# New step costs, a delay for each engine and later weight landings in the list schedule of an experts' stage

## The chip, the core and the metric

The kernel runs on one core of one Trainium2 chip. The metric is the time of one launch on the device, in microseconds (us). Before the change three runs took 1431.03, 1432.60 and 1433.58 us; the median is 1432.6 us. The execution that was profiled is the one of 1433.58 us.

## The reference

Three parts follow each other: linear attention, a layer of eight experts with fixed capacity, and a wide feed-forward layer. All of it is float32.

```python
q_s = softmax(q, axis=-1); k_s = softmax(k, axis=2)          # (8, 8, 576, 64)
kv  = einsum('bhsd,bhse->bhde', k_s, v)
x   = einsum('bhsd,bhde->bhse', q_s, kv) -> reshape (4608, 512)

logits = x @ w_gate                                          # 4608 x 8
for idx in argsort(-logits.flatten()):                       # greedy, best pair first
    tok, e = idx // 8, idx % 8
    if assigned[tok] >= 0 or counts[e] >= 576: continue
    assigned[tok] = e; counts[e] += 1
for e in range(8):
    out[assigned == e] = maximum(x[assigned == e] @ w1[e], 0) @ w2[e]   # 512 -> 1024 -> 512

h = out @ w_in                                               # 512 -> 2048
y = (h * tanh(softplus(h))) @ w_out                          # 2048 -> 512
```

The greedy assignment fills the experts one after another: each expert ends up with exactly 576 tokens.

## The kernel before, in words

Three stages stand behind each other in time: attention with the first list of tokens (to about 170 us of the span), the eight experts (about 172 to 670 us), and the feed-forward layer, called block 2 here (from about 660 us to the end). The change concerns the experts' stage.

**What the experts' stage does.** For each expert a list of its 576 tokens must be found, its tokens gathered from HBM, transposed and multiplied.

- `route(ph)` makes the list of expert `ph`. It is one long chain between VectorE (DVE) and TensorE (PE): six rounds, each of a compare on DVE (`cmp`, tile `cm`), 18 small matmuls that count (L868), two DVE instructions for flags, one matmul that broadcasts (L879), and two DVE instructions. Then `place`, `onehot`, 18 matmuls (L792), four matmuls (L807), and `ids`, which writes the list `ix` (L812, L814). Lists 1 to 7 are made in this stage, while earlier experts are multiplied. Expert 0's list is made in the attention stage.
- `load_x(ph)` gathers the tokens by the list in five indirect DMAs, issued by GpSimd (POOL) (tile `xg`, L952), transposes each on PE (four matmuls, tile `tp`, L963) and splits the result into a high part (ScalarE, ACT, L969) and a low part (DVE, L973), tile `xT`. There is one PSUM buffer `tp`, so a transposition can't start before the low part of the one before is made.
- `load_expert(ph)` gathers the weights in eight indirect DMAs on POOL (tile `wst`, four buffers, L924) and splits each half into high (ACT, L905) and low (DVE, L911), tile `unit`.
- `expert(ph)` is the bulk of PE's work: 16 hops of 24 matmuls each, 128x288 out. Each hop's result goes through ACT (`hh`, L1001) and DVE (`hh`, L1005), and back to PE (`yp`, L1013). ACT also writes the result out (`ys`, L1020).
- `convert_w` rewrites the weights of block 2 (from 64-bit words to high and low parts) on ACT and DVE and stores them in HBM with DMAs from SyncE's queue (SP; L1211, L1240), in gaps of the same stage.

**What sets the order.** Class `Sched` takes every step of the stage with an engine, a cost in us, its reads and writes, a priority and a count of buffers. `run()` (L92) plays a clock: it takes the step that can start first (ties by priority), books its engine for `cost`, and lets its readers start `lat` later. The Python functions of the steps are called in that order, so the clock's order is the order of instructions in each engine's queue. An engine takes its queue strictly in that order: an instruction that waits holds all that stand behind it. No time of this clock is in the program; it only sets the order.

- `lat` is one number in this stage before: 0.259 us. A DMA from SP has 2.53 us, a gather its own `lat=` (tokens 5.0 us, weights 5.5 us; expert 0: 3.0 and 4.0).
- `keep` (0.332 before): if a step of low priority on DVE or ACT would be taken, and a step of high priority would become ready within `keep` times its cost, the latter is taken instead (L115 to L121).
- `slack` adds to the ready time of a step: 0.3 us for PE's steps of `route`.

The last 17 steps of the experts and block 2 have schedulers of their own.

Of the kernel before, what the change touches and what calls it, by code (L numbers as in the profile page):

```python
# [23 lines left out]
NJ = NT // 128  # L24
# [12 lines left out]

LISTS = 5.7


class Sched:
# [39 lines left out]
    def run(self, free=()):  # L81
# [28 lines left out]
        while ready:  # L110
# [497 lines left out]
class Moe:  # L608
# [17 lines left out]
    def route(self, ph, bank):  # L626
# [76 lines left out]
        def rows():  # L703
# [4 lines left out]
            if not last:  # L708
                V.tensor_tensor(c["act"], c["act"], T["est"], op=OP.subtract)
        dve(0.7, expert, r=["acc", ("act", 0)] + allv + ([] if last else [f"nb{NR - 1}"]), w=["est"])  # L710

        def select():
# [8 lines left out]
            V.scalar_tensor_tensor(sel[:, 1], T["x"][:, :, 0], T["ns"], cs, op0=OP.is_equal, op1=OP.mult)  # L721
        dve(0.8, select, r=["est", "acc"] + allv, w=["sel"])
        dve(0.6, rows, r=["est"], w=["wi", ("act", 0)])

# [50 lines left out]
        def pay():  # L775
# [5 lines left out]
            for a in range(2):  # L781
                V.tensor_tensor(P[:, :, a], b, two(c["thl"][:, a])[:, :, None, :].to_broadcast(sh), op=OP.mult)
        dve(1.1, pay, r=["qr"], w=["P"])
        CH = [(0, 9), (9, 18)] if ph == 0 else [(0, 18)]
        for g0, g1 in CH:
            dve(0.08 + 0.073 * (g1 - g0), lambda g0=g0, g1=g1: onehot(g0, g1), r=["qr"], w=["A%d" % g0] + (["A"] if g0 == 0 else []))

# [7 lines left out]
        for g0, g1 in CH:  # L795
            pe(0.03 * (g1 - g0), lambda g0=g0, g1=g1: lists(g0, g1), r=["A", "A%d" % g0, "P"], w=["ls"],
               new=["ls"] if g0 == 0 else [])
# [12 lines left out]
        def ids():  # L810
# [3 lines left out]
            V.scalar_tensor_tensor(ix, T["sp"][:, 0:5], 64.0, lh, op0=OP.mult, op1=OP.add)  # L814
        dve(0.22, flat, r=["ls"], w=["iv"])
        pe(0.15, spread, r=["iv"], w=["sp"], new=["sp"])
        dve(0.38, ids, r=["sp"], w=["ix"])

# [12 lines left out]
        if not last:  # L831
            def done():
                V.scalar_tensor_tensor(L, T["est"][:, None, :].to_broadcast([128, NJ, E]), -BIG, L,
                                       op0=OP.mult, op1=OP.add)
            p += 5
            dve(0.5, done, r=["est"] + (["ix"] if ph == 0 else []), w=[("L", 0)] + ([("L", j) for j in range(1, NJ)] if ph == 0 else []))

    def keep_list(self, ph):
        self.sc.op("POOL", 0.6, self.keep[ph], r=[("ix", ph)], w=[("gl", ph)], prio=0, slack=0.0 if ph else LISTS + 10.0)

    def round(self, ph, T, n, dve, pe, bank, cuts, allw, allv):
# [47 lines left out]
        for j0, j1 in CH:  # L889
            dve(0.16 + 0.00053 * NT_ * (j1 - j0), lambda j0=j0, j1=j1: cmp(j0, j1), r=["w%d" % j0, "cm"][:2 if j0 else 1] if first else allw + ["cm"] * (j0 > 0) + ["acc"] * (n > 0) + [("ls", ph - 1)] * (n == 0 and ph > 0),  # L890
                w=["cm%d" % j0] + ["cm"] * (j0 == 0), early=first and j1 < NJ)
# [24 lines left out]
    def load_expert(self, ph, w1, w2, xd):  # L916
# [11 lines left out]
        for which, rows in (("w1", w1r), ("w2", w2r)):  # L928
            for g in range(4):
                key = (which, ph, g)  # L930
                first = ph == 0 and which == "w1"
                sc.op("POOL", 1.1, lambda w=which, g=g, r=rows: weight(w, g, r),
                      r=[("wi", ph)] + ([("xg", 0, 4)] if ph == 0 and which == "w2" else []), w=[key],
                      new=[("wst", key)], prio=-2001 if first else p, lat=4.0 if first else 5.5)
                for q in range(2):
# [10 lines left out]
    def load_x(self, ph, xd):  # L946
# [28 lines left out]
        for t in range(5):  # L975
            n = 128 if t < 4 else 64
            xg, tp, xt = ("xg", ph, t), ("tp", ph, t), ("xt", ph, t)
            sc.op("POOL", 1.1 if ph else 1.25, lambda t=t, n=n: gather(t, n), r=[("ix", ph), "xd"], w=[xg], new=[("xg", xg)],
                  prio=p, lat=5.0 if ph else 3.0, slack=0.0 if ph else LISTS)
            sc.op("PE", 0.45 if ph else 0.85, lambda t=t, n=n: tr(t, n), r=[xg], w=[tp], new=[("tp", tp)] if ph or t == 4 else [], prio=p)  # L980
            sc.op("ACT", 0.61, lambda t=t, n=n: hi(t, n), r=[tp] + ([("xT", ph)] if t else []), w=[xt] + ([("xT", ph)] if t == 0 else []),
                  new=[("xT", ("xT", ph))] if t == 0 else [], prio=p)
            sc.op("DVE", 0.7, lambda t=t, n=n: low(t, n), r=[tp, xt, ("xT", ph)], w=[xt], prio=p)

    def expert(self, ph, yd):
# [50 lines left out]
        for hf in range(2):  # L1036
            for f in range(8):
                hp, hh = ("hp", ph, hf, f), ("hh", ph, hf, f)

                def hop(hf=hf, f=f, hp=hp, hh=hh):  # L1040
# [5 lines left out]
                    over = ph == E - 1 and hf == 1 and f >= 8 - OVER  # L1046
                    self.sc.op("ACT", 0.43, lambda: h_hi(hf, f), r=[hp], w=[hh], new=[("unit" if over else "hh", hh)], prio=-5000)
                    self.sc.op("DVE", 0.47, lambda: h_lo(hf, f), r=[hp], w=[hh], prio=-5000)

                def yop(hf=hf, f=f, hh=hh):  # L1050
# [10 lines left out]
                    elif f == 7:  # L1061
                        for d in range(4):
                            self.sc.op("ACT", 0.43, lambda d=d: y_out(hf, d), r=[yp] + ([("ys", ph, hf)] if d else []),
                                  w=[("ys", ph, hf, d)] + ([("ys", ph, hf)] if d == 0 else []),
                                  new=[("ys", ("ys", ph, hf))] if d == 0 else [], prio=-4000)
# [77 lines left out]
    def convert_w(self, w_in, w_out, wdo, wdi):  # L1143
# [9 lines left out]
        def load(key, src, behind=(), unit=False):  # L1153
# [16 lines left out]
            p, gate = when()  # L1170
            sc.op("DMA", 2.6, ld, r=gate, w=[k64], new=[("w64", k64)], prio=p, lat=4.0)
            sc.op("ACT", 0.69, size, r=[k64] + list(behind), w=[cv], new=[("unit" if unit else "cv", cv)], prio=p)
            for step in range(3):
                sc.op("DVE", (0.45, 0.72, 0.72)[step], lambda step=step: bits(step), r=[k64], w=[cv], prio=p)
            return cv

        def split(cv, key, store, done):
# [13 lines left out]
            count[0] += 1  # L1191
            sc.op("ACT", 0.66, hi, r=[cv], w=[uw], new=[("unit", uw)] if cv != uw else [], prio=p)
            sc.op("DVE", 0.71, low, r=[cv, uw], w=[uw], prio=p)
            sc.op("DMA", 2.6, lambda: store(T["uw", key]), r=[uw], w=[done], prio=p)

        def combine(name, out, a, b, op, fresh=False):
# [349 lines left out]
def attention_moe_ffn(ctx, tc, q, k, v, w_gate, w1, w2, w_in, w_out, out):  # L1546
# [106 lines left out]
```

## Time and profile before

| | |
|---|---|
| median of three runs | 1432.6 us |
| the profiled execution, its own time | 1433.58 us |
| its span, first to last instruction | 1431.8 us |
| mean granted TensorE clock | 0.975 |
| PE busy, DVE busy, ACT busy, POOL busy | 94%, 73%, 55%, 19% |
| matmuls | 10256 |

The profile page gives the busy share of each engine, and the queries of the trace give rows for stretches of the span. PE's busy time runs from a matmul's start to a modelled end, so matmuls that follow each other overlap. A busy PE is therefore not PE at its peak; what tells more is the idle time in front of an instruction, which a row gives in brackets with what ended it. The granted clock stands in each stretch as a share of 2.4 GHz; 0.5 is the lower level, 1.2 GHz. In the order of instructions times don't occur at all; they are read from the trace.

### The profile page before, as it was taken

Reading aid. Unit: us, or ns where it says so; the run is one execution under the profiler, and the core shown is the slowest. Engines: PE = TensorE matmul, PEld = TensorE weight load, DVE = VectorE, ACT = ScalarE, POOL = GpSimd, SP = SyncE. Lnnn points to the kernel's source line nnn. Section 1 sums busy time; section 2 is a strip of 40 time slices with the busy share of each in tenths; the row PEclk is TensorE's granted clock in tenths of the full one; section 3 lists DMA queues with packets and bytes.
Section 4 is the critical chain, followed back from the end, with each engine's and each line's share of the span. In section 5 each row is a group of like instructions: output and inputs, shape, how many; then the busy total and the mean of one; then the engine's idle time right before and its main releaser. Section 6 shows DMA issues by size and latency. Waiting matters only on the chain.

```text
span 1431.8 us, 26732 instructions
## 1 busy us (share of the span) xinstructions
PE 1344.6 (94%) x10256; PEld 1244.2 (87%) x10256; DVE 1046.1 (73%) x2207; ACT 790.8 (55%) x1513; POOL 277.1 (19%) x314
## 2 busy tenths in 40 slices
PE   4987399999999789998999999999999999999997
PEld 4877298999999789998889989899898998999996
DVE  7897768887878757746787686776768677786764
ACT  4675224343344336434666666666666666675663
POOL 7896213312322231100001010000101001010101
PEclk9999599999999889999999999999999999999999
DMA  9997325555556668767966676675658556665650
GB/s 259 268 259 282 129 61 169 171 169 153 161 185 195 202 204 274 243 210 251 351 199 216 185 216 180 203 241 177 213 173 256 175 185 206 212 210 171 202 169 30
DMA packets 161919, 286.98 MB, mean 200 GB/s; under 512 B 25600, under 2 KB 101376, under 8 KB 161792
## 3 DMA queue, kind: packets, MB, share of 16 engines
q1 hardware_dynamic: 137680, 222.35, 51.1%
q0 software_dynamic: 15040, 52.44, 11.1%
q10 hardware_dynamic: 9072, 10.49, 2.1%
q8 instruction: 81, 1.33, 0.4%
q14 instruction: 46, 0.38, 0.1%
HBM read 235.95 MB, written 49.28 MB: 199 GB/s over the span
## 4 chain that ended last, share of the span: by engine, by line
PE 55%; issue 30%; DMA 5%; DVE 5%; POOL 2%; ACT 2%; SPq 1%; ACTq 0%; POOLq 0%; DVEq 0%
PE hp L994 13%; PE yp L1013 12%; PE yp L1479 12%; PE hp L1353 11%; PE rt L868 2%; DMA kh<-in_k_dram 2%; POOL out_dram L1491 2%; DMA wst<-in_moe_w_dram,wi 2%; PE tp L963 1%; PE xp L429 1%; DMA xg<-xd,ix 1%; DVE km L244 1%; DMA v<-in_v_dram 1%; DMA q<-in_q_dram 0%; DVE cm L856 0%
## 5 line engine op out<-in xcount | busy, mean ns | idle before, releaser
L1479 PE MATMUL yp<-unit,g 128*128 128x512 f32 x1728 | 431.3, 392 | 0.1
L1479 PEld LDWEIGHTS yp<-unit,g 128*128 128x128 f32 x1728 | 309.9, 188 | 56.4 <-DVE g L1391 1.0
L1353 PEld LDWEIGHTS hp<-yTa,unit 128*128 128x128 f32 x2256 | 288.3, 188 | 18.6 <-DVE hp L1442 2.9
L1353 PE MATMUL hp<-yTa,unit 128*128 128x256 f32 x2256 | 294.0, 279 | 4.1 <-DVE hp L1442 2.7
L994 PE MATMUL hp<-xT,unit 128*128 128x288 f32 x1536 | 284.7, 303 | 4.2 <-DVE hh L1005 3.5
L1013 PE MATMUL yp<-hh,unit 128*128 128x288 f32 x1500 | 266.6, 297 | 0.0
L994 PEld LDWEIGHTS hp<-xT,unit 128*128 128x128 f32 x1536 | 229.8, 191 | 5.3 <-DVE hh L1005 4.1
L1013 PEld LDWEIGHTS yp<-hh,unit 128*128 128x128 f32 x1500 | 222.2, 189 | 0.4 <-ACT ys L1020 0.2
L1491 POOL DMA_INDIRECT out_dram<-os,gix x36 | 38.6, 1073 | 793.8 <-ACT os L1487 454.6
L1001 ACT ACTIVATE hh<-hp 128x288 fp32r<-128x288 f32 x125 | 51.3, 411 | 199.3 <-PE hp L994 183.3
L1361 ACT ACTIVATE u<-hp 128x512 f32<-128x512 f32 x144 | 86.1, 598 | 117.7 <-PE hp L1353 112.4
L1378 DVE SCALAR_TENSOR_TENSOR u<-w,r 128x512 f32<-128x512 f32 x144 | 98.7, 687 | 45.5 <-ACT r L1375 44.9
L1388 ACT ACTIVATE g<-w 128x512 fp32r<-128x512 f32 x144 | 90.3, 627 | 74.8 <-DVE w L1384 74.0
L924 POOL DMA_INDIRECT wst<-in_moe_w_dram,wi x64 | 66.7, 1043 | 259.4 <-DVE unit L911 54.1
L1005 DVE SCALAR_TENSOR_TENSOR hh<-hp,hh 128x288 fp32r<-128x288 f32 x125 | 56.6, 455 | 71.1 <-ACT hh L1001 70.9
L905 ACT ACTIVATE unit<-wst 128x512 fp32r<-128x512 f32 x128 | 77.9, 645 | 55.5 <-DMA wst<-in_moe_w_dram,wi 51.1
L1391 DVE TENSOR_TENSOR g<-w,g 128x512 fp32r<-128x512 f32 x144 | 98.8, 686 | 5.6 <-ACT g L1388 4.1
L1384 DVE SCALAR_TENSOR_TENSOR w<-r,hp 128x512 f32<-128x512 f32 x144 | 98.3, 683 | 5.5
L1353 PEld LDWEIGHTS hp<-yTb,unit 128*128 128x128 f32 x768 | 99.1, 191 | 3.5
L1353 PE MATMUL hp<-yTb,unit 128*128 128x256 f32 x768 | 102.1, 282 | 0.0
L1381 DVE SCALAR_TENSOR_TENSOR r<-u,r 128x512 f32<-128x512 f32 x144 | 98.8, 687 | 1.9
L1364 DVE TENSOR_SCALAR u<-u 128x512 f32<-128x512 f32 x144 | 61.0, 425 | 51.0 <-ACT u L1361 50.4
(205 smaller groups left out, 1724.1 us busy)
## 6 DMA issues: line engine op xcount, KB each, us to landing
unit<-wdi SPq DMA_DIRECT2D x216, 512.0 KB, 4.2
unit<-wdi SPq DMA_DIRECT2D x72, 256.0 KB, 3.9
wdi<-unit SPq DMA_DIRECT2D x56, 256.0 KB, 3.4
yd<-ys ACTq DMA_DIRECT2D x15, 576.0 KB, 5.2
k<-in_k_dram SPq DMA_DIRECT2D x16, 512.0 KB, 6.4
q<-in_q_dram SPq DMA_DIRECT2D x16, 512.0 KB, 7.0
v<-in_v_dram SPq DMA_DIRECT2D x32, 256.0 KB, 6.3
xd<-xs SPq DMA_DIRECT2D x16, 512.0 KB, 4.4
```

The costliest lines, as they stand in the source:

```text
L905: nc.scalar.activation(f, v, AF.Copy)
L994: MM(t, u[:, a, 128 * (f % 4):128 * (f % 4) + 128], x[:, b, k, HALF * hf:HALF * hf + HALF], start=(k == 0 and n == 0), stop=(k == 3 and n ...
L1013: MM(T["yp", ph, hf][d], u[:, a, 128 * d:128 * d + 128], t[:, b], start=(f == 0 and n == 0), stop=(f == 7 and n == 2))
L1353: MM(dst, u[:, h, a, kk], y[:, b, kk], start=first, stop=False, skip_group_check=True)
L1361: nc.scalar.activation(t, T[zp], AF.Exp)
L1378: V.scalar_tensor_tensor(T[u], T[w], 1.0, T[rk], op0=OP.add, op1=OP.mult)
L1381: V.scalar_tensor_tensor(T[rk], T[u], 2.0, T[rk], op0=OP.subtract, op1=OP.mult)
L1384: V.scalar_tensor_tensor(T[w], T[rk], 0.5, T[zp], op0=OP.add, op1=OP.mult)
L1388: nc.scalar.activation(t[:, 0], T[w], AF.Copy)
L1391: V.tensor_tensor(T[g][:, 1], T[w], T[g][:, 0].bitcast(F32), op=OP.subtract)
L1479: MM(T["op", c, t], g[:, a, 128 * t:128 * t + 128], u[:, b], start=(i == 0 and n == 0), stop=(i == 15 and n == 2))
L1491: at = nc.gpsimd.indirect_dma_start(out=out, out_offset=bass.IndirectOffsetOnAxis(ap=gix[:, 4 * c + t:4 * c + t + 1], axis=0), in_=T["os", ...
```

## The change

It replaces numbers that `Sched` reckons with, in the experts' stage. `lat` becomes a table by engine (PE 0.23, DVE 0.14, ACT 0.16, POOL 0.25), `keep` goes from 0.332 to 1.0, the costs of the steps on DVE, ACT and PE become smaller by 0.04 to 0.3 us (a few become larger: the gathers on POOL from 1.1 to 1.25 us, the first DVE steps of lists 1 to 7), and the landing of a weight gather goes from 5.5 to 8.0 us. The landing of a token gather stays at 5.0 us. The steps themselves, their instructions, buffers and priorities stay as they are. The schedules of the attention stage and of block 2 give the same order of instructions as before. The diff, cut to its core:

```diff
+LAT = {"PE": 0.23, "DVE": 0.14, "ACT": 0.16, "POOL": 0.25}
+KEEP = 1.0
...
-            done = e + (lat if lat is not None else 2.53 if eng == "DMA" else self.lat)
+            done = e + (lat if lat is not None else 2.53 if eng == "DMA" else self.lat if isinstance(self.lat, float) else self.lat[eng])
...
-            dve(0.7 + 0.05 * (j1 - j0), lambda ...: sel_first(j0, j1), ...
+            dve(0.7 + 0.05 * (j1 - j0) if ph == 0 else 2.28, lambda ...: sel_first(j0, j1), ...
...
-        dve(1.7, place, r=["sl", "unsel"], w=["qr", ("fs", 0)])
+        dve(1.45, place, r=["sl", "unsel"], w=["qr", ("fs", 0)])
...
-        dve(0.33, flags, r=[c4], w=[fl])
-        pe(0.15, bcast, r=[fl], w=[nb], new=[nb])
-        dve(0.5 if n + 1 < NR else 0.18, accum, r=[nb] + allw, w=["acc"])
+        dve(0.28, flags, r=[c4], w=[fl])
+        pe(0.06, bcast, r=[fl], w=[nb], new=[nb])
+        dve(0.4 if n + 1 < NR else 0.1, accum, r=[nb] + allw, w=["acc"])
...
-        sc.op("ACT", 0.66, hi, r=[key], w=[unit, hk], new=[("unit", unit)], prio=prio)
-        sc.op("DVE", 0.71, low, r=[key, hk, unit], w=[lk], prio=prio)
+        sc.op("ACT", 0.56, hi, r=[key], w=[unit, hk], new=[("unit", unit)], prio=prio)
+        sc.op("DVE", 0.61, low, r=[key, hk, unit], w=[lk], prio=prio)
...
-                sc.op("POOL", 1.1, lambda w=which, g=g, r=rows: weight(w, g, r), ...
-                      new=[("wst", key)], prio=-2001 if first else p, lat=4.0 if first else 5.5)
+                sc.op("POOL", 1.25, lambda w=which, g=g, r=rows: weight(w, g, r), ...
+                      new=[("wst", key)], prio=-2001 if first else p, lat=4.0 if first else 8.0)
...
-                    self.sc.op("ACT", 0.43, lambda: h_hi(hf, f), ...
-                    self.sc.op("DVE", 0.47, lambda: h_lo(hf, f), ...
+                    self.sc.op("ACT", 0.32, lambda: h_hi(hf, f), ...
+                    self.sc.op("DVE", 0.38, lambda: h_lo(hf, f), ...
...
-    sc = m.sc = Sched(slots, 0.259, 0.332)
+    sc = m.sc = Sched(slots, LAT, KEEP)
```

Line numbers of the changed kernel are four higher than those of the kernel before, from L43 on.

**Two places in the order.** The first is ACT's queue around the transpositions of list 1 (`xT`), the weight splits (`unit<-wst`), the results of expert 0 that are written out (`ys`), and the converted weights of block 2 (`cv`). Before:

```order
L1020 ACTIVATE ys<-yp_2759 128x288
L905 ACTIVATE unit<-wst 128x512
L1020 ACTIVATE ys<-yp_2760 128x288
L1020 ACTIVATE ys<-yp_2761 128x288
L1020 ACTIVATE ys<-yp_2762 128x288
L969 ACTIVATE xT<-tp 128x4x128
L1028 DMA yd_61<-ys 128x4x288
L905 ACTIVATE unit<-wst 128x512 x4
L969 ACTIVATE xT<-tp 128x4x128
```

The same list in the changed kernel, on the same engine, from its first transposition to its last:

```order
L973 ACTIVATE xT<-tp 128x4x128
L1097 ACTIVATE cv<-w_2911 128x512
L1005 ACTIVATE hh<-hp 128x288
L973 ACTIVATE xT<-tp 128x4x128 x2
L909 ACTIVATE unit<-wst 128x512
L1005 ACTIVATE hh<-hp 128x288
L909 ACTIVATE unit<-wst 128x512 x5
L973 ACTIVATE xT<-tp 128x4x128
L973 ACTIVATE xT<-tp 128x4x64
```

The transpositions of list 1 stood between and behind the `ys` of expert 0 and the splits of the weights. Now three of the five stand ahead of those splits, and the `ys` have moved away behind them.

The second is PE's queue at list 6, from its last matmuls (L807) to the transposition of the first tokens gathered by it (L963). Before:

```order
L807 LDWEIGHTS lst
L807 MATMUL rt<-iv,lst 128x10
L994 MATMUL hp<-xT,unit 128x288 x3
L1013 MATMUL yp_6585<-hh,unit 128x288 x3
L1013 MATMUL yp_6586<-hh,unit 128x288 x3
L735 LDWEIGHTS tri
L735 MATMUL rt<-rk,tri 128x2
L736 LDWEIGHTS irt
L736 MATMUL rt<-rk,irt 128x1
L963 MATMUL tp<-ident,xg 128x128 x4
```

In the changed kernel list 6 is made some 50 us of matmuls earlier, and 11.6 us of matmuls stand between its L811 and its first transposition. Its second and third transposition, in the hops of expert 5, with all that lies between:

```order
L967 MATMUL tp<-ident,xg 128x128 x4
L998 MATMUL hp<-xT,unit 128x288 x3
L1017 MATMUL yp_6755<-hh,unit 128x288 x3
L998 MATMUL hp<-xT,unit 128x288 x3
L1017 MATMUL yp_6752<-hh,unit 128x288 x3
L998 MATMUL hp<-xT,unit 128x288 x3
L1017 MATMUL yp_6753<-hh,unit 128x288 x3
L998 MATMUL hp<-xT,unit 128x288 x3
L1017 MATMUL yp_6754<-hh,unit 128x288 x3
L967 MATMUL tp<-ident,xg 128x128 x4
```

Before, nine matmuls of the experts and two small ones lay between list and transposition, and none of the experts' matmuls between the first and the second transposition of list 6. Now 24 of them lie between one transposition and the next.

## Rows read from the trace of the kernel before

**Rows 1.** The page, part 4: the chain that ended last, by engine.

```profile
PE 55%; issue 30%; DMA 5%; DVE 5%; POOL 2%; ACT 2%; SPq 1%; ACTq 0%; POOLq 0%; DVEq 0%
```

**Rows 2.** Windows of 10 us: busy us by engine (instructions), clock, DMA share, GB/s.

```profile
230.00:240.00 10.00, 9.65 (x109) 8.88 (x108) 8.01 (x21) 3.87 (x8) 7.16 (x7) 1.00 0.69 220
240.00:250.00 10.00, 7.63 (x72) 6.98 (x69) 7.56 (x19) 6.36 (x14) 0.00 (x0) 0.83 0.37 136
...
330.00:340.00 10.00, 7.95 (x64) 7.50 (x63) 6.17 (x14) 2.20 (x5) 7.28 (x7) 0.83 0.70 197
...
490.00:500.00 10.00, 1.94 (x26) 1.67 (x24) 6.36 (x18) 2.27 (x5) 6.80 (x6) 0.68 0.83 279
500.00:510.00 10.00, 8.63 (x48) 7.70 (x49) 9.15 (x18) 5.40 (x11) 4.78 (x6) 0.64 0.48 137
510.00:520.00 10.00, 7.47 (x57) 7.23 (x57) 3.87 (x8) 2.21 (x5) 6.14 (x7) 1.00 0.88 292
520.00:530.00 10.00, 10.00 (x65) 10.00 (x66) 7.77 (x14) 3.99 (x8) 1.87 (x2) 0.83 0.86 294
530.00:540.00 10.00, 10.00 (x78) 10.00 (x77) 1.42 (x4) 2.93 (x9) 0.00 (x0) 1.00 0.08 31
```

**Rows 3.** The same view, one window of 50 us.

```profile
250.00:300.00 50.00, 50.00 (x465) 48.63 (x464) 41.19 (x107) 19.84 (x42) 13.63 (x15) 1.00 0.51 163
```

**Rows 4.** Waits in 180 to 670 us: total us, times, longest.

```profile
PE tp L963 <- DMA xg<-xd,ix: 9.3, 2, 7.3
...
PE hp L994 <- DVE hh L1005: 3.5, 2, 2.5
...
ACT unit L905 <- DMA wst<-in_moe_w_dram,wi: 20.5, 13, 7.6
```

**Rows 5.** PE by time: start, us, instruction, in brackets idle before, releaser.

```profile
243.10 0.66 PE L963 MATMUL tp<-ident,xg 128*128 128x128 f32 x4 [1.60 <-DVE xT L973]
...
325.45 0.26 PE L807 MATMUL rt<-iv,lst 128*128 128x10 bf16 x4
...
336.63 1.12 PE L963 MATMUL tp<-ident,xg 128*128 128x128 f32 x4 [2.05 <-DMA xg<-xd,ix]
...
488.48 0.26 PE L807 MATMUL rt<-iv,lst 128*128 128x10 bf16 x4
...
497.33 1.11 PE L963 MATMUL tp<-ident,xg 128*128 128x128 f32 x4 [7.25 <-DMA xg<-xd,ix]
...
519.84 0.66 PE L994 MATMUL hp<-xT,unit 128*128 128x288 f32 x3 [2.53 <-DVE hh L1005]
```

**Rows 6.** ACT in order of time, at the stall of 241 us.

```profile
240.30 0.63 ACT L905 ACTIVATE unit<-wst 128x512 fp32r<-128x512 f32 x1 [0.72 <-DMA wst<-in_moe_w_dram,wi]
...
241.71 0.61 ACT L969 ACTIVATE xT<-tp 128x512 fp32r<-128x512 f32 x1
```

**Rows 7.** POOL by time, before token gathers of lists 3 and 6.

```profile
330.30 0.18 POOL L823 COPY gix<-ix 64x4 int32<-64x4 int32 x1 [3.11 <-DMA wst<-in_moe_w_dram,wi]
...
489.91 1.29 POOL L952 DMA_INDIRECT xg<-xd,ix  x1 [0.39 <-PE yp L1013]
```

**Rows 8.** Token gathers (L952): us from issue to landing.

```profile
DMA to landing us min/median/max: 3.1/4.1/8.4
```

**Rows 9.** Weight gathers (L924): the same.

```profile
DMA to landing us min/median/max: 4.1/5.4/8.7
```

**Rows 10.** The chain in order of time: start, us, piece.

```profile
252.34 0.65 PE rt L868 x18
...
255.99 0.79 PE yp L1013 x6
```

**Rows 11.** DVE in order of time: runs of equal instructions.

```profile
182.22 0.81 DVE L1005 SCALAR_TENSOR_TENSOR hh<-hp,hh 128x288 fp32r<-128x288 f32 x2
...
502.25 1.89 DVE L911 TENSOR_TENSOR unit<-wst,unit 128x512 fp32r<-128x512 f32 x3
```

**Rows 12.** SP by time: the last store of converted weights.

```profile
623.38 10.64 SPq L1240 DMA_DIRECT2D wdo<-unit  x2
```

More of the change, by code (lines that the diff above doesn't have):

```diff
@@ L709, in rows @@
                 V.tensor_tensor(c["act"], c["act"], T["est"], op=OP.subtract)
-        dve(0.7, expert, r=["acc", ("act", 0)] + allv + ([] if last else [f"nb{NR - 1}"]), w=["est"])
+        dve(0.6, expert, r=["acc", ("act", 0)] + allv + ([] if last else [f"nb{NR - 1}"]), w=["est"])
         def select():
@@ L795, in route @@
         for g0, g1 in CH:
[L796 removed]
+            pe(0.027 * (g1 - g0), lambda g0=g0, g1=g1: lists(g0, g1), r=["A", "A%d" % g0, "P"], w=["ls"],
                new=["ls"] if g0 == 0 else [])
@@ L835, in route @@
             p += 5
-            dve(0.5, done, r=["est"] + (["ix"] if ph == 0 else []), w=[("L", 0)] + ([("L", j) for j in range(1, NJ)] if ph == 0 else []))
+            dve(0.36, done, r=["est"] + (["ix"] if ph == 0 else []), w=[("L", 0)] + ([("L", j) for j in range(1, NJ)] if ph == 0 else []))
     def keep_list(self, ph):
-        self.sc.op("POOL", 0.6, self.keep[ph], r=[("ix", ph)], w=[("gl", ph)], prio=0, slack=0.0 if ph else LISTS + 10.0)
+        self.sc.op("POOL", 0.7, self.keep[ph], r=[("ix", ph)], w=[("gl", ph)], prio=0, slack=0.0 if ph else LISTS + 10.0)
     def round(self, ph, T, n, dve, pe, bank, cuts, allw, allv):
@@ L931, in load_expert @@
                 first = ph == 0 and which == "w1"
-                sc.op("POOL", 1.1, lambda w=which, g=g, r=rows: weight(w, g, r),
+                sc.op("POOL", 1.25, lambda w=which, g=g, r=rows: weight(w, g, r),
                       r=[("wi", ph)] + ([("xg", 0, 4)] if ph == 0 and which == "w2" else []), w=[key],
-                      new=[("wst", key)], prio=-2001 if first else p, lat=4.0 if first else 5.5)
+                      new=[("wst", key)], prio=-2001 if first else p, lat=4.0 if first else 8.0)
                 for q in range(2):
@@ L980, in load_x @@
             sc.op("PE", 0.45 if ph else 0.85, lambda t=t, n=n: tr(t, n), r=[xg], w=[tp], new=[("tp", tp)] if ph or t == 4 else [], prio=p)
-            sc.op("ACT", 0.61, lambda t=t, n=n: hi(t, n), r=[tp] + ([("xT", ph)] if t else []), w=[xt] + ([("xT", ph)] if t == 0 else []),
+            sc.op("ACT", 0.5 if t < 4 else 0.3, lambda t=t, n=n: hi(t, n), r=[tp] + ([("xT", ph)] if t else []), w=[xt] + ([("xT", ph)] if t == 0 else []),
                   new=[("xT", ("xT", ph))] if t == 0 else [], prio=p)
-            sc.op("DVE", 0.7, lambda t=t, n=n: low(t, n), r=[tp, xt, ("xT", ph)], w=[xt], prio=p)
+            sc.op("DVE", 0.61 if t < 4 else 0.35, lambda t=t, n=n: low(t, n), r=[tp, xt, ("xT", ph)], w=[xt], prio=p)
     def expert(self, ph, yd):
@@ L1046, in hop @@
                     over = ph == E - 1 and hf == 1 and f >= 8 - OVER
-                    self.sc.op("ACT", 0.43, lambda: h_hi(hf, f), r=[hp], w=[hh], new=[("unit" if over else "hh", hh)], prio=-5000)
-                    self.sc.op("DVE", 0.47, lambda: h_lo(hf, f), r=[hp], w=[hh], prio=-5000)
+                    self.sc.op("ACT", 0.32, lambda: h_hi(hf, f), r=[hp], w=[hh], new=[("unit" if over else "hh", hh)], prio=-5000)
+                    self.sc.op("DVE", 0.38, lambda: h_lo(hf, f), r=[hp], w=[hh], prio=-5000)
                 def yop(hf=hf, f=f, hh=hh):
@@ L1062, in yop @@
                         for d in range(4):
-                            self.sc.op("ACT", 0.43, lambda d=d: y_out(hf, d), r=[yp] + ([("ys", ph, hf)] if d else []),
+                            self.sc.op("ACT", 0.31, lambda d=d: y_out(hf, d), r=[yp] + ([("ys", ph, hf)] if d else []),
                                   w=[("ys", ph, hf, d)] + ([("ys", ph, hf)] if d == 0 else []),
@@ L1170, in load @@
             p, gate = when()
-            sc.op("DMA", 2.6, ld, r=gate, w=[k64], new=[("w64", k64)], prio=p, lat=4.0)
-            sc.op("ACT", 0.69, size, r=[k64] + list(behind), w=[cv], new=[("unit" if unit else "cv", cv)], prio=p)
+            sc.op("DMA", 1.8, ld, r=gate, w=[k64], new=[("w64", k64)], prio=p, lat=5.0)
+            sc.op("ACT", 0.58, size, r=[k64] + list(behind), w=[cv], new=[("unit" if unit else "cv", cv)], prio=p)
             for step in range(3):
-                sc.op("DVE", (0.45, 0.72, 0.72)[step], lambda step=step: bits(step), r=[k64], w=[cv], prio=p)
+                sc.op("DVE", (0.36, 0.62, 0.62)[step], lambda step=step: bits(step), r=[k64], w=[cv], prio=p)
             return cv
@@ L1191, in split @@
             count[0] += 1
-            sc.op("ACT", 0.66, hi, r=[cv], w=[uw], new=[("unit", uw)] if cv != uw else [], prio=p)
-            sc.op("DVE", 0.71, low, r=[cv, uw], w=[uw], prio=p)
-            sc.op("DMA", 2.6, lambda: store(T["uw", key]), r=[uw], w=[done], prio=p)
+            sc.op("ACT", 0.54, hi, r=[cv], w=[uw], new=[("unit", uw)] if cv != uw else [], prio=p)
+            sc.op("DVE", 0.61, low, r=[cv, uw], w=[uw], prio=p)
+            sc.op("DMA", 1.8, lambda: store(T["uw", key]), r=[uw], w=[done], prio=p)
         def combine(name, out, a, b, op, fresh=False):
@@ L1201, in combine @@
             p, _ = when()
-            sc.op("DVE", 0.71, go, r=[a, b], w=[out], new=[("cv", out)] if fresh else [], prio=p)
+            sc.op("DVE", 0.61, go, r=[a, b], w=[out], new=[("cv", out)] if fresh else [], prio=p)
         def part(cv, what, q, kk):
```

26 lines of the change are left out of this document (13 added, 13 removed).

## The prediction, made before the changed kernel was run

> **What bounds the kernel now.** I read the page's chain first: PE carries 55% of what ended last and "issue" 30%, DVE and ACT together 7% [rows 1]. A chain so full of PE says that the time is PE's work plus the holes in it, so the second view is the one of windows, 10 us at a time through the experts' stage. In a good window PE is busy for all 10.00 us at a granted clock of 1.00 with 78 matmuls, as in 530 to 540 [rows 2]. Seven others are not. Per window I count as lost the idle time, and of the busy time the part that the clock withheld, (10 − busy) + busy × (1 − clock):
>
> - 230 to 240: 0.35; 240 to 250: 2.37 + 7.63 × 0.17 = 3.67
> - 330 to 340: 2.05 + 7.95 × 0.17 = 3.40
> - 490 to 500: 8.06 + 1.94 × 0.32 = 8.68; 500 to 510: 1.37 + 8.63 × 0.36 = 4.48
> - 510 to 520: 2.53; 520 to 530: 10.00 × 0.17 = 1.70
>
> The sum is **24.8 us**, all from [rows 2]. In each case the clock falls below 1.00 only in a window with a hole or in the one behind it, so I treat it as part of the hole's price.
>
> Third, the waits of the stage tell who makes the holes. PE's transpositions wait for tokens for 9.3 us in two waits; ACT's weight splits wait for gathered weights for 20.5 us in 13, up to 7.6 [rows 4]. Then the engines in order of time, hole by hole:
>
> - **Hole A, 238 to 243.** ACT waits for a weight gather before a split [rows 6]. Behind that split, in ACT's queue, stand the results of expert 0 and the split of list 1's transposition, so PE's next transposition starts only at 243.10, 1.60 us late [rows 5].
> - **Hole B, 334 to 337.** List 3 leaves PE at 325.45, its first transposition waits 2.05 us for its tokens [rows 5]. POOL held them up: the copy in front of the token gathers waited 3.11 us for the landing of a weight gather [rows 7].
> - **Hole C, 490 to 510.** List 6 leaves PE at 488.48, POOL issues its first gather at 489.91, and PE, whose queue has next to nothing before the transposition, stands idle for 7.25 us [rows 5, 7]. The transpositions then follow each other at the low clock.
> - **Hole D, 517 to 520.** 2.53 us before a hop whose `hh` is late [rows 5], which is again queued behind late weights.
>
> **The change, part by part.** No instruction is added or removed, and nothing changes in attention, or in block 2 except when its first work can start. So the sum is made of which hole the new order closes, and which it opens. Distances in the order I turn into time with the trace's own durations: six 288-column matmuls take 0.79 us, 0.132 each, and 18 counting matmuls 0.65 [rows 10].
>
> *Lists earlier, and gathers with room.* From a list's last matmuls to its first transposition there lie, lists 1 to 7, 8.1, 9.3, 8.9, 8.5, 8.1, 1.3 and 7.3 us of PE work before and 8.1, 8.1, 8.9, 9.3, 8.1, 11.6 and 50.5 us now. What is needed is 1.43 us to the issue (488.48 to 489.91 [rows 5, 7]) and a landing of 3.1, 4.1 or 8.4 us (minimum, median, maximum [rows 8]), so 4.5, 5.5 or 9.8. List 6, with 1.3, had to fail; with 11.6 it is safe even at the maximum. That closes hole C. It is also made some 48 us of PE work earlier, and list 7 39 us earlier. Hole B closes for another reason. Its distance doesn't grow, but the copy before list 3's gathers now waits only for gathers that were issued over 38 us of PE work earlier, where before one stood 3.3 us ahead of it; for lists 1 and 5 the nearest is 14 us back. Four of the lists still have only 8.1 to 8.9 us, though, less than the 9.8 of the worst landing. I leave **2.0 us** for that: one transposition that meets a maximum (9.8 − 8.1 = 1.7) and a little clock behind it.
>
> *Later weight landings.* Weights take 4.1, 5.4 or 8.7 us to land [rows 9]; half of them were later than the 5.5 that the plan had. In the order before, the PE work between a gather's issue and its split on ACT goes down to between 2 and 6 us in eight places. Now it is 9.5 us or more, except for two gathers of expert 0 (5.9 and 7.6). That is more than the largest landing, so the 20.5 us of ACT's waits [rows 4] should mostly go, and holes A and D with them. The same reading of the order says that the weights of expert 5, which were made 0.5 us ahead of their use, are now made 24 us ahead.
>
> The Trainium skill (page "DMA: Bandwidth & Descriptors", section "Anatomy of one DMA — SWDGE (gpsimd) path") gives 2.0 us plus the bytes at 436 GB/s for such a transfer. For a weight gather of 512 KB that would be an estimate of 3.2 us, and for 256 KB of tokens 2.6 us. The trace has medians of 5.4 and 4.1 and maxima of 8.7 and 8.4 [rows 8, 9], so here the measurement decides; by the page the delay of 8.0 us would buy nothing, which is the third rival below.
>
> *Transpositions further apart.* One `tp` buffer means PE's transposition, ACT's split and DVE's in a row: 0.66 [rows 5], 0.61 [rows 6] and about 0.605 (between starts of the run of three in [rows 11]), some 1.9 us. Before, the closest pairs had 0.6 to 1.3 us of PE work from one to the next; now 1.8 to 2.7. I leave **0.5 us**.
>
> *Smaller costs, a wider `keep`.* Equal instructions on DVE follow each other at 0.36 to 0.38 us (`hh`; the run of two takes 0.81) and 0.605 us (splits; the run of three takes 1.89) [rows 11]. The new costs are 0.38 and 0.61, the old ones 0.47 and 0.71: the plan ran DVE some 0.1 us per step too slow, and now packs it as the chip does. What it pays for that is cover. The PE work between the steps of a list's chain shrinks (median of flags to broadcast 1.58 to 1.19 us, compare to count 3.16 to 2.44, DVE's split to the next transposition 2.6 to 2.2), at 102 places. Each still holds more than one DVE step that could get in the way, so I cost them at nothing but **1.5 us** together, for single ones and for a few weight units that are now just in time (1.6 to 5 us ahead).
>
> *The end of the stage.* The last of block 2's converted weights leaves SP's queue at 623.38 + 10.64 = 634.0 [rows 12], where block 2's first work stands at about 661. That leaves 27 us. Its place in the order moves from 420.7 to 410.9 us of PE work, so it stays hidden when the stage ends 21 us sooner.
>
> **The sum.** 24.8 − (2.0 + 0.5 + 1.5) = 20.8 us gained. The profiled execution took 1433.58 us, its span 1431.8 and 1.8 around it; it would take 1412.8. It lies 1.0 above the median of the runs, so I forecast **1412 us**. For the unknown terms: if the 4.0 us left over are nothing and some small holes outside the seven windows close too, 1404; if they are three times as large, 1420.
>
> **The rivals.**
>
> *Crowded conversions.* The conversions move: 34 instead of 26 of their stores lie between 248 and 347 us of PE work, on a DVE that was already busy 41.2 of 50 us at 250 to 300 [rows 3]. If `hh` and the lists' steps queue behind them, single holes of the size of D, A and their clock come back. I price it at 4.5 + 2.5 + 1.7 = 8.7 us, the windows of 500, 510 and 520: 1412 + 8.7 = 1421. Against it: what moves in is taken from places around it, and the splits no longer hold ACT.
>
> *The hole only moves.* Hole C might have been the weights of expert 5 and not the tokens. DVE is still making weight splits at 502 [rows 11], in the middle of the hole. Then 490 to 510 stays with 8.68 + 4.48, the gain is 24.8 − 13.2 − 4.0 = 7.6, and the time 1425. Against it: PE's row names tokens, and the order has those weights 24 us ahead now.
>
> *The planned landings make no difference.* If gathers land well ahead of their splits once POOL has issued them, ACT's waits come from late issues, and a plan that reckons with later landings changes nothing. Holes A and D then stay, with 0.35 + 3.67 + 2.53 + 1.70 = 8.25; the gain is 24.8 − 8.25 − 4.0 = 12.6, the time 1420. A median landing of 5.4 us [rows 9] speaks against it. The formula of the Trainium skill's page cited above speaks for it.
>
> *No change.* Were block 2's start set by its weights, the stage could end sooner and nothing be gained: 1430 to 1435. The 27 us of slack speak against it.
>
> *Slower: thin cover.* The 102 places with less cover each come late, because one `hh` step of 0.37 us [rows 11] gets in front. That costs 102 × 0.37 = 37.7 us, more than the 24.8: 1432.6 + 12.9 = 1446. It decides from 24.8 / 102 = 0.24 us a place. DVE's high load in the lists' windows speaks for it, the remaining cover of over 1 us against it.
>
> **Chances.** The forecast 0.62; crowded conversions 0.14; the hole moves 0.08; planned landings without effect 0.03; no change 0.06; slower 0.07. What a measurement of this kernel can tell from no change is about 0.2%, 2.9 us. Faster is the first four, 0.87; the same 0.06; slower 0.07. The range for 8 in 10 takes the forecast's own 1404 to 1420, a little below, and up to past the moved hole: **1403 to 1428**.
>
> **What would show it.** In the profile after, PE's transpositions wait for token gathers under 3 us in all, ACT's L909 for weights close to nothing. No window between 190 and 650 falls below 9 us of PE or a clock of 0.9, and block 2 starts some 21 us sooner and takes as long as before. It would be wrong if a hole of several us stands somewhere else with `hh`, `unit` or `xT` as its releaser (crowding, a moved hole), or if the stage is full of waits below 0.5 us behind flags and accumulations (thin cover).

## The result, and the profile after

The changed kernel takes 1419.5 us (median of 6 runs, 1417.4 to 1421.0); the kernel before took 1433.1 in its 6 runs beside it. The ratio is 0.9902, 95% interval 0.9887 to 0.9917, so the change gains 13.6 us. The forecast was 1412, the range 1403 to 1428. The profiled execution took 1418.27 us with a span of 1416.5, 15.3 less than the one of before; it is a little below its median, as the one of before was a little above.

Of the 15.3 us 15.2 lie ahead of block 2. Its first matmuls of L1353, now L1357, in the kernel before and in the changed one:

```profile
660.98 1.57 PE L1353 MATMUL hp<-yTa,unit 128*128 128x256 f32 x12
```

```profile
645.75 1.56 PE L1357 MATMUL hp<-yTa,unit 128*128 128x256 f32 x12
```

From there to the end both take 770.8 us. The view of windows, with columns as in [rows 2], shows the stage after:

```profile
230.00:240.00 10.00, 10.00 (x105) 9.54 (x104) 7.96 (x22) 5.13 (x10) 1.89 (x3) 1.00 0.56 205
240.00:250.00 10.00, 10.00 (x92) 9.52 (x91) 8.59 (x33) 4.46 (x11) 1.86 (x2) 1.00 0.15 50
...
300.00:310.00 10.00, 9.16 (x98) 8.64 (x97) 9.32 (x22) 2.44 (x8) 5.63 (x6) 1.00 0.33 102
310.00:320.00 10.00, 8.59 (x92) 8.07 (x90) 6.64 (x17) 5.45 (x12) 6.20 (x6) 1.00 1.00 309
...
370.00:380.00 10.00, 9.54 (x98) 8.77 (x98) 8.48 (x21) 6.22 (x14) 0.94 (x1) 1.00 0.83 239
...
480.00:490.00 10.00, 6.73 (x46) 6.50 (x46) 7.42 (x15) 7.54 (x15) 1.98 (x2) 0.91 0.88 281
490.00:500.00 10.00, 10.00 (x73) 9.96 (x72) 7.37 (x15) 5.52 (x13) 3.92 (x4) 0.92 0.89 301
...
540.00:550.00 10.00, 8.05 (x63) 7.77 (x61) 8.48 (x17) 7.35 (x17) 0.98 (x1) 1.00 1.06 321
```

Holes A (238 to 243) and D (517) of [rows 2] are gone, and PE is full through what was hole C, except for a new hole at 480 to 490. By the formula of the prediction the losses are 0.84 + 1.41 at 300 to 320, 0.46 at 370, 3.88 + 0.80 at 480 to 500 and 1.95 at 540: **9.3 us**, where before there were 24.8. The difference, 15.5, is the gain of the profiled execution within 0.3 us. The forecast had left 4.0. So the question is where the other 5.3 us come from. The waits of 180 to 655 us answer it:

```profile
ACT unit L909 <- DMA wdi<-unit: 9.7, 6, 2.1
...
ACT unit L1190 <- DMA wdi<-unit: 6.2, 3, 3.1
...
PE tp L967 <- DVE xT L977: 5.7, 3, 3.3
...
PE tp L967 <- DMA xg<-xd,ix: 2.3, 2, 1.4
...
PE hp L998 <- DVE hh L1009: 0.2, 1, 0.2
...
ACT unit L909 <- DMA wst<-in_moe_w_dram,wi: 0.5, 1, 0.5
```

Against [rows 4] ACT's waits for gathered weights fell from 20.5 us to 0.5 and PE's for tokens from 9.3 to 2.3. New are ACT's waits for `wdi<-unit`, a DMA that writes converted weights of block 2 to HBM: 15.9 us in nine waits. In the kernel before the same view has these two lines for it, 2.5 us in two waits:

```profile
ACT unit L905 <- DMA wdi<-unit: 1.8, 1, 1.8
...
ACT unit L1186 <- DMA wdi<-unit: 0.7, 1, 0.7
```

Why a split of weights waits for a store: both use the 24 buffers `unit`. A converted weight lies in one until its store has landed, and the next split takes that buffer. ACT in order of time at the largest hole:

```profile
481.28 1.14 ACT L909 ACTIVATE unit<-wst 128x512 fp32r<-128x512 f32 x2
484.50 0.66 ACT L909 ACTIVATE unit<-wst 128x512 fp32r<-128x512 f32 x1 [2.09 <-DMA wdi<-unit]
485.07 0.40 ACT L1005 ACTIVATE hh<-hp 128x288 fp32r<-128x288 f32 x1
485.36 0.59 ACT L973 ACTIVATE xT<-tp 128x512 fp32r<-128x512 f32 x1
```

The split at 484.50 waits for a store; a hop's `hh` and list 6's transposition stand behind it. DVE then makes the low part of that transposition, and only then is `tp` free for PE:

```profile
487.21 0.66 PE L967 MATMUL tp<-ident,xg 128*128 128x128 f32 x4 [3.27 <-DVE xT L977]
```

It is hole A's form again, ACT's queue held by a split, with a store instead of a gather in front. The hole at 542 is the same. The one at 300 to 320 is list 3's, on POOL:

```profile
300.03 1.11 POOL L928 DMA_INDIRECT wst<-in_moe_w_dram,wi  x1 [14.15 <-DVE ix L818]
301.19 0.23 POOL L826 COPY gix<-ix 64x5 int32<-64x5 int32 x1
304.63 0.65 POOL L827 COPY gix<-ix 64x4 int32<-64x4 int32 x1 [3.21 <-DMA wst<-in_moe_w_dram,wi]
```

Here the reader sees [rows 7] once more: a weight gather is issued just before the list's copies, the copy waits 3.21 us for its landing (3.11 before), and the token gathers stand behind the copy.

### The profile page after: what moved, and what is told of

Read it like the earlier page. It is cut to its first block, busy times and chain, and to the rows that moved or that the text cites. A ratio compares the mean times of both kernels' runs of the same rounds, so it can differ in the third digit from the quotient of the medians.

```text
span 1416.5 us, 26771 instructions
## 1 busy us (share of the span) xinstructions
PE 1336.9 (94%) x10256; PEld 1236.3 (87%) x10256; DVE 1047.9 (74%) x2207; ACT 789.9 (56%) x1513; POOL 275.8 (19%) x314
## 4 chain that ended last, share of the span: by engine, by line
PE 56%; issue 28%; DMA 5%; DVE 4%; POOL 3%; SPq 2%; ACT 2%; ACTq 0%; POOLq 0%; DVEq 0%
PE hp L998 14%; PE yp L1017 13%; PE yp L1483 12%; PE hp L1357 11%; PE rt L872 2%; POOL out_dram L1495 2%; DMA kh<-in_k_dram 1%; DMA wdi<-unit 1%; PE tp L967 1%; DMA q<-in_q_dram 1%; PE xp L433 1%; SPq L212 1%; DMA xg<-xd,ix 1%; DMA v<-in_v_dram 1%; DVE cm L860 0%
## 5 line engine op out<-in xcount | busy, mean ns | idle before, releaser
L1357 PEld LDWEIGHTS hp<-yTa,unit 128*128 128x128 f32 x2256 | 288.4, 188 | 18.5 <-DVE hp L1446 2.9
L1357 PE MATMUL hp<-yTa,unit 128*128 128x256 f32 x2256 | 294.1, 280 | 4.1 <-DVE hp L1446 2.7
L1357 PEld LDWEIGHTS hp<-yTb,unit 128*128 128x128 f32 x768 | 99.2, 191 | 3.6
L1357 PE MATMUL hp<-yTb,unit 128*128 128x256 f32 x768 | 102.1, 283 | 0.0
```

Source lines behind the costliest of these rows:

```text
L1357: MM(dst, u[:, h, a, kk], y[:, b, kk], start=first, stop=False, skip_group_check=True)
```

## The experiments

Four kernels ran on one chip, four on a second, four on a third, each set beside runs of the kernel before. On the second chip the latter took 1442.1 us (1434.6 to 1450.6), so kernels of different sets are compared by ratio, not by time. Theory S is that the stores' planned landing makes the new holes, P that the copy on POOL makes list 3's, L that the gathers' planned landing makes the gain. The rivals are C (a crowd of conversions), K (the costs and `keep` make the gain), R (slow transfers) and Z (every new order makes new holes of about the same sum).

**Landing of the gathers back at 5.5 (e2), and that alone in the kernel before (e3).**

```diff
-  prio=-2001 if first else p, lat=4.0 if first else 8.0)   # changed kernel
+  prio=-2001 if first else p, lat=4.0 if first else 5.5)   # e2
-  prio=-2001 if first else p, lat=4.0 if first else 5.5)   # kernel before
+  prio=-2001 if first else p, lat=4.0 if first else 8.0)   # e3
```

> The changed kernel with the planned landing of a weight gather back at 5.5 us; all else of the change stays. Theory L (the longer landing takes away ACT's waits for gathered weights): these waits in 180 to 655 us go back up from 1.3 us to 10 us or more, and 3 to 9 us of the gain are lost, 1423 to 1429. Rival K (the gain comes from the smaller costs and keep, which moved list 6): the time stays within 3 us of the changed kernel, 1417 to 1422, though ACT waits longer.

> The kernel before with only the planned landing of a weight gather at 8.0 us instead of 5.5. Theory L: ACT's waits for gathered weights fall from 20.5 us to under 5 and the holes at 238 to 243 and 517 go (8.3 us), the one at 490 to 510 stays or not by the chance of the order: 1424 without its going, 1412 to 1418 with it. Rival K: no gain without the new costs, 1430 to 1436.

e2: 1431.2 us, ratio 0.9983 (0.9964 to 1.0001). Its waits in 180 to 655:

```profile
PE tp L967 <- DVE xT L977: 11.2, 6, 3.7
...
ACT unit L1190 <- DMA wdi<-unit: 9.0, 4, 4.2
ACT unit L909 <- DMA wst<-in_moe_w_dram,wi: 8.6, 7, 2.9
ACT unit L909 <- DMA wdi<-unit: 7.5, 6, 3.9
```

e3: 1424.3 us, 0.9935 (0.991 to 0.996). Its windows at the old holes, and its waits for weights:

```profile
240.00:250.00 10.00, 6.45 (x60) 5.73 (x57) 5.79 (x15) 4.26 (x9) 2.06 (x2) 0.83 0.79 267
490.00:500.00 10.00, 10.00 (x81) 9.86 (x80) 5.78 (x24) 2.44 (x7) 5.03 (x7) 1.00 0.57 190
500.00:510.00 10.00, 9.47 (x89) 9.00 (x88) 8.75 (x20) 3.88 (x8) 6.21 (x6) 1.00 0.72 228
520.00:530.00 10.00, 6.19 (x40) 5.96 (x39) 4.82 (x10) 3.85 (x10) 3.77 (x4) 0.81 0.92 294
```

```profile
ACT unit L905 <- DMA wst<-in_moe_w_dram,wi: 14.1, 5, 6.9
```

Without the longer landing all other numbers together gain 0.2%, not clear of nothing, although list 6 is as early there as in the changed kernel (its L811 at 440.9, against 436.3 after and 488.5 before). Rival K falls. But e2 lost more than the 3 to 9 us expected, and not by weights alone. One hole of 4.9 us, at 320 to 330, stands for the most part behind a wait for weights; those of 4.1 us at 500 to 520 and 5.9 at 550 to 560 stand behind these waits for stores:

```profile
506.06 0.66 ACT L909 ACTIVATE unit<-wst 128x512 fp32r<-128x512 f32 x1 [3.89 <-DMA wdi<-unit]
...
549.53 0.63 ACT L1190 ACTIVATE unit<-cv 128x512 fp32r<-128x512 f32 x1 [4.23 <-DMA wdi<-unit]
```

So e2 shows that the gain needs the longer landing, but its loss is no price of the waits for weights.

The landing alone gains 9 us, more than half, but not as expected: ACT still waits 14.1 us for weights (under 5 expected), hole A stays, 6.5 us at 520 to 540 stand in hole D's place, and it is hole C that closes, with list 6 as late as before. Its first transposition now stands 8.7 us behind the list, and PE doesn't wait for it:

```profile
492.64 0.26 PE L807 MATMUL rt<-iv,lst 128*128 128x10 bf16 x4
...
501.38 0.60 PE L963 MATMUL tp<-ident,xg 128*128 128x128 f32 x4
```

Neither part cures the waits for weights alone: 20.5 us before, 14.1 with the landing, 8.6 with the other numbers, 0.5 with both. Why 8.0 us didn't suffice in e3 can be seen at one of its waits, in ACT's split and in the gather that it waits for, on POOL:

```profile
247.95 0.63 ACT L905 ACTIVATE unit<-wst 128x512 fp32r<-128x512 f32 x1 [3.56 <-DMA wst<-in_moe_w_dram,wi]
```

```profile
240.25 0.95 POOL L924 DMA_INDIRECT wst<-in_moe_w_dram,wi  x1 [0.30 <-issue]
```

From issue to split it is 7.70 us, less than the 1.1 + 8.0 that this plan has, so the gather itself left late by the plan. Ahead of it on POOL a copy had stood for 3.00 us, and most token gathers left 1.25 us apart, where the plan has 1.1. Which of the two counts no run separates.

**`keep` back at 0.332 (e4).** `KEEP = 1.0` becomes `KEEP = 0.332`.

> The changed kernel with keep back at 0.332. By theory L and theory S keep carries nothing: 1416 to 1423, with the waits for weights as small as in the changed kernel (under 4 us). By rival K, if keep is the part that protects the lists and hops, hh steps come late behind splits: more small waits of PE on DVE, 1424 or more.

1417.0 us, 0.9887 (0.9859 to 0.9914), the changed kernel within its uncertainty. ACT waits 2.5 us for weights. `keep` carries nothing that can be measured, though the holes lie elsewhere: none at 480, and 5.8 us at 400 to 420, where PE waits 3.00 us for tokens.

**Stores planned to land later (e1, again as e10, and e12).**

```diff
-            sc.op("DMA", 1.8, lambda: store(T["uw", key]), r=[uw], w=[done], prio=p)
+            sc.op("DMA", 1.8, lambda: store(T["uw", key]), r=[uw], w=[done], prio=p, lat=8.0)    # e12: 10.0
```

> The changed kernel, with one number more: the store of a converted weight is planned to land 8.0 us after its issue step instead of 2.53. Theory S (the two holes that the changed kernel has at 484 to 487 and 542 to 544 come from unit buffers that are planned free before their store has landed): ACT's waits for stores of converted weights fall from 15.9 us (9 waits) to under 4, both holes close, and with 4.7 + 2.0 us less the time is 1411 to 1415. Rival C (the holes are made by the crowd of conversions on DVE and ACT, whichever buffer they use): the waits for stores shrink, but holes of 2 us or more in front of transpositions stay, 1417 to 1422. A hole of about 2 us at list 3 (copy on POOL) stays by both.

> The kernel with the planned landing of stores at 8.0 us, beside the changed one. Theory S: 3 to 6 us faster than the changed kernel on the same chip, ACT's waits for stores under 6 us, no hole at 542. Rival Z (a new order makes as much as it takes): within 2 us of it.

> The changed kernel with stores planned to land after 10.0 us, the copies left where the change has them. Theory S: ACT's waits for stores under 3 us, neither of the two holes; 4 to 8 us faster than the changed kernel on the same chip. If longer planned landings only push conversions into the next list (rival Z), PE waits behind DVE grow instead and it is no faster than the one with 8.0.

> The changed kernel itself, on one chip with the three kernels below, since the gains at stake (2 to 6 us) are smaller than the differences between chips. It should stand at 0.988 to 0.992 of the kernel before, with the holes at 300 to 320, 484 to 487 and 542 to 544 and some 16 us of ACT's waits for stores.

e1 took 1416.3 us (1412.8 to 1419.5), 0.9887 (0.986 to 0.9915), too wide to tell from the changed kernel; e10 is the same kernel again. On the third chip all stood side by side, 6 runs each: the changed kernel (e9) 1421.0 (1418.4 to 1423.9), ratio 0.9901 (0.9878 to 0.9924); e10 1414.5 (1409.0 to 1416.2), 0.985 (0.9825 to 0.9875); e12 1413.7 (1408.6 to 1415.9), 0.9845 (0.982 to 0.9871). So on this chip the later landing gains 6.5 and 7.4 us on top of the change; no run of e10 or e12 is as slow as the fastest of e9. By e1's ratio it would be some 2 us: that it gains is shown on one chip, how much stays open. ACT's waits for stores, of e9 and then of e12:

```profile
ACT unit L1190 <- DMA wdi<-unit: 9.7, 5, 4.6
ACT unit L909 <- DMA wdi<-unit: 7.5, 6, 2.5
```

```profile
ACT unit L909 <- DMA wdi<-unit: 3.0, 1, 3.0
...
ACT unit L1190 <- DMA wdi<-unit: 2.2, 1, 2.2
...
ACT unit L909 <- DMA wst<-in_moe_w_dram,wi: 1.4, 2, 0.8
...
ACT unit L1097 <- DMA wdi<-unit: 0.9, 1, 0.9
```

17.5 us (with 0.3 for another store) became 6.1 in e12, where under 3 was expected, and 5.2 in e10, where under 6 was. The hole at 542 is gone in e1, e10 and e12. The one at 480 stays, by one last wait of 2 to 3 us, where the expectations of e1 and e12 had none. In e12, the wait and the windows:

```profile
480.83 0.66 ACT L909 ACTIVATE unit<-wst 128x512 fp32r<-128x512 f32 x1 [3.02 <-DMA wdi<-unit]
```

```profile
480.00:490.00 10.00, 7.62 (x48) 7.39 (x47) 6.38 (x12) 5.34 (x11) 3.14 (x4) 0.83 0.93 333
540.00:550.00 10.00, 10.00 (x79) 9.77 (x78) 7.58 (x16) 8.25 (x18) 0.94 (x1) 1.00 0.76 267
```

Theory S holds for the waits and for the hole at 542; of that at 480 the stores' wait is the cause, but the number alone doesn't remove it. Rivals C and Z fall here: DVE and ACT are busy for 346 to 348 and 194 to 196 us of 180 to 640 in e9, e10 and e12 alike, and the sum of holes did shrink. By the formula 180 to 630 loses 14.5 us in the profiled execution of e9 and 6.5 in e10's and e12's. About half of the 8.0 comes at 480 to 500 (7.5 us in e9, 3.1 and 3.7 then). Of e9's 7.5 the clock took 3.0; in the first profile of the same kernel it took 1.4 there, so some of the 8.0 is chance.

**Two other knobs on the same waits (e11, e7).** e11 tells the planner of 23 `unit` buffers (`"unit": NU - 1`); e7 puts the conversions' DMA numbers back as they were before.

```diff
-            sc.op("DMA", 1.8, ld, ..., lat=5.0)
+            sc.op("DMA", 2.6, ld, ..., lat=4.0)
-            sc.op("DMA", 1.8, lambda: store(T["uw", key]), ...
+            sc.op("DMA", 2.6, lambda: store(T["uw", key]), ...
```

> The changed kernel, with the planner told of one unit buffer less (23 of the 24 that there are); stores are planned to land after 2.53 us as in the change. Theory S by another knob: a buffer's next split is planned against an older store, so ACT's waits for stores fall from 15.9 us to under 8 and the holes behind them shrink, 1413 to 1418 where the changed kernel has 1419. Rival: buffers are then short for the weights, ACT's and POOL's gathers come later, waits of ACT or PE for weights appear and the time is 1420 or more.

> The changed kernel with only the conversions' DMA numbers as they were before (2.6 us a load and a store, landing of a load 4.0). Theory S: with stores planned 0.8 us longer, ACT's waits for stores fall from 15.9 us to between 4 and 10, and the two holes shrink: 1413 to 1418. If the shorter numbers (1.8 us) have no part in those waits, they stay at 12 us or more and the time at 1418 to 1422.

e11: ACT's waits for stores fell to 7.9 us (under 8 expected), a hole of 4.2 stayed at 540; 1418.9 us, 0.9889 (0.9867 to 0.9911), not to be told from e9. e7: these waits fell to 6.1 us (4 to 10 expected), with other holes at 310 to 330 (5.7 us) and 540 (3.3); ratio 0.9833 (0.9773 to 0.9894), on the second chip, too wide to place against 0.99. Both knobs move the waits as theory S says, and neither shows a gain of its own.

**The copies behind the gathers (e5, e6, e8).** The list's copies are planned 8 us later; e6 has the stores at 8.0 with it, e8 at 10.0.

```diff
-        self.sc.op("POOL", 0.7, self.keep[ph], ..., prio=0, slack=0.0 if ph else LISTS + 10.0)
+        self.sc.op("POOL", 0.7, self.keep[ph], ..., prio=0, slack=8.0 if ph else LISTS + 10.0)
```

> The changed kernel with POOL's two copies of a list (L826, L827) planned 8 us later, so that they stand behind the token gathers of the same list. Theory P (list 3's tokens are late because the copy in front of their gathers waits for the weight gather issued just before): POOL's copy waits no longer stand ahead of token gathers, PE's waits for tokens fall from 2.3 us to under 0.5 and the holes at 300 to 320 (2.25 us) close; with the holes by stores left alone the time is 1415 to 1419. Rival R (the tokens are late because transfers are slow there, DMA share 1.00): the waits for tokens at list 3 stay, 1418 to 1423.

> Both of these: the store of a converted weight planned to land 8.0 us after its issue step, and the list's copies 8 us later. If theories S and P are both right, ACT's waits for stores are under 5 us and PE's waits for tokens under 0.5 in all, and 5 to 8 us go against the changed kernel: 1410 to 1414. If the chance of the order decides (rival Z: every new order makes new holes of about the same sum), 1415 to 1420 with holes at other places.

> As the one with both, but the store planned to land after 10.0 us instead of 8.0. Theory S: stores landed up to 8.4 us after issue in the run with 8.0 and ACT still waited 4.3 us for them; with 10.0 that wait is under 2 us. Time 1409 to 1414; by rival Z 1415 to 1420.

POOL in e5: list 3's gathers now go first, and the copy waits 8.01 us further back, where nothing of list 3 stands behind it.

```profile
298.31 0.95 POOL L956 DMA_INDIRECT xg<-xd,ix  x1 [1.01 <-PE hp L998]
...
317.74 0.59 POOL L827 COPY gix<-ix 64x4 int32<-64x4 int32 x1 [8.01 <-DMA wst<-in_moe_w_dram,wi]
```

PE doesn't wait for tokens any more in any of the three, so P is right about the cause of those waits, and R, by which they would stay, falls. But e5 loses 2.0 us at 300 to 320 all the same: there a list's counting matmuls now wait for their compare, as in e6 and e8 (1.6 us each).

```profile
312.34 0.80 PE L872 MATMUL rt<-C,cm 128*128 128x16 bf16 x18 [1.57 <-DVE cm L860]
```

No gain shows in the times: e5 0.9917 (0.989 to 0.9945), e6 0.9876 (0.9809 to 0.9942, too wide for either side), e8 0.9912 (0.9879 to 0.9946). The windows of e5 have new holes of 6.7 us at 350 to 370 and 6.1 at 540 to 560; e8 has 4.8 us at 260 and 6.4 at 400 to 420, where PE waits 3.91 and 3.75 us for a list's flags. ACT's waits for `wdi<-unit` came to 6.0 us in e6 (under 5 expected) and 6.1 in e8 (under 2). For the copies rival Z fits e5 and e8: the edit shuffles the order elsewhere and makes as much as it takes. For e6 it stays open: its profiled execution, the fastest of its four, loses 6.8 us at 180 to 630, about as much as e10's.

## Why the prediction was right, and where not

**The mechanism was right for the holes that were there.** The losses were the holes of seven windows. Holes A, C and D closed, by later planned landings together with the other numbers (which of these count is not shown, but for `keep`, which doesn't), and the stage ended sooner by what they had cost less what is left. ACT's waits for weights went to 0.5 us. Block 2 did not cap the gain: the last store of converted weights now leaves SP's queue at 608.9 us, 37 ahead of it. But block 2 starts 15.2 us sooner, not 21.

```profile
598.44 10.48 SPq L1244 DMA_DIRECT2D wdo<-unit  x3
```

**Signs of being wrong came too.** PE falls below 9 us in three windows (8.59, 6.73 and 8.05), where the prediction allowed none, and the 3.27 us before 487.21 have `xT` as their releaser, its sign of crowding. By the time alone 1419.5 lies nearer to the 1421 of crowded conversions and the 1420 of the planned landings than to 1412; only the windows and waits tell them apart.

**The step that was mis-sized is what is left over: 9.3 us instead of 4.0.** Its three terms:

- *Transpositions, 0.5 us.* With their clock they cost 7.1 us (0.46 + 3.88 + 0.80 + 1.95). The prediction looked for them in the chain of `tp`; of the three, the two large ones waited behind a split that waited for a store. The description of the change leaves out the conversions' own DMA numbers (a load or a store 2.6 us, now 1.8; the landing of a load 4.0, now 5.0), and the prediction did not price them at all. A store was planned at 2.6 + 2.53 = 5.1 us from start to landing and became 1.8 + 2.53 = 4.3, while the profile page, issue to landing (us in the last column), says first of before and then of after:

```profile
wdi<-unit SPq DMA_DIRECT2D x56, 256.0 KB, 3.4
```

```profile
wdi<-unit SPq DMA_DIRECT2D x56, 256.0 KB, 5.3
```

  The plan became shorter where the transfers became longer. Why they did is not shown; the median is 5.0 in e10 and 3.7 in e12.
- *Landings of tokens, 2.0 us.* The size is right (2.25) by luck, since the reason is wrong. The prediction said that list 3's copy now waits only for gathers far back. The order had a gather right ahead of the copies, the one at 300.03, as near as the one of before, and it was overlooked. Hole B did not close; it shrank from 3.40 us to 2.25, since the clock stayed at 1.00 this time.
- *Thin cover, 1.5 us.* There was nothing: PE has no wait on a list's flags or compares in the stage (one of 0.8 us before). The 1.5 us left for it made up for some of the transpositions'.

Two readings were off besides. The plan's 5.5 us count from the end of a gather's step, the trace's 5.4 from its start. Against 1.1 + 5.5 = 6.6 us only 8 of the 46 gathers whose landing the trace has were late, not half; the new 1.25 + 8.0 = 9.25 lies above the largest, 9.0. And outside the seven windows the kernel before loses only 1.3 us between 180 and 660, so the small holes there could not bring 1408 down to the 1404 of the range.

**The rivals.** *Crowded conversions* came half true: 8.7 us were priced, the holes by conversions cost 6.6. But not through DVE, where it was looked for: they hold buffers until their stores land, and ACT's queue waits. *The hole only moves* was wrong in its cause (expert 5's weights), yet a smaller hole stands at 480. *Planned landings without effect* is refuted by e2 and e3, though its reason, gathers that leave late, is what e3 shows at 247.95. The gathers land as before, 4.2, 5.4 and 9.0 us for weights. The formula of the Trainium skill's page ("DMA: Bandwidth & Descriptors", section "Anatomy of one DMA — SWDGE (gpsimd) path"), with an estimate of 3.2 us for such a transfer, doesn't describe them here. *No change* and *slower* did not come.

**Hole C closed by the distance, not by the early list.** The prediction gave both: more PE work between list and transposition, and a list made earlier. In e3 the list is as late as ever and its first transposition stands 8.7 us behind it, which suffices. In e2 the list is early and PE doesn't wait for its tokens either, but other holes took the time.

## What to carry to other kernels

When a list schedule sets the order, look up every planned time that frees a buffer or lets a reader start, stores included. Count it from the same point as the trace does, and hold it against the slow end of what the trace measures, not its median: an in-order queue turns one late transfer into a stall of all that stands behind it. Here only values below the slow end (5.5, 2.53) and near or above it (8.0, 10.0) were run, none between. Costs that equal the measured spacing are worth little as long as landings are planned too early; here all numbers but the gathers' landing gained 2 us without it, not clear of nothing, and some 5 on top of it. And a single edit to such a plan reorders much else, so compare the waits that it was meant to remove as well as the time.

## What was not expected of the hardware

The price of a hole depends on the clock behind it. In the changed kernel's two profiles PE's wait near 485 is 3.3 us and 4.0 us long. In 480 to 500 the granted clock was 0.91 and 0.92 in the first, which took 1.4 us from PE, and in the second (e9) it took 3.0:

```profile
480.00:490.00 10.00, 6.63 (x49) 6.17 (x47) 7.21 (x15) 5.66 (x13) 1.93 (x2) 0.99 1.02 298
490.00:500.00 10.00, 8.84 (x49) 8.80 (x50) 7.30 (x14) 5.73 (x13) 3.12 (x3) 0.67 0.80 259
```

The same kernel before took 1433 us on one chip, 1435 on another and 1442 on a third, with runs up to 16 us apart there, so that gains of 5 us show only side by side. The version with the stores at 10.0 us (e12, 1413.7 us) beats both kernels; with 8.0 it is the same within the uncertainty.
